# A batch's first expert block: transposed in one slot, begun in the next

## The chip, the cores and the metric

The kernel runs on one core of a Trainium2 chip. Its time is the device time of one execution in microseconds (us). The kernel before takes 1374.13 us (median of three runs, 1373.11 to 1375.44). One further execution was recorded by the hardware profiler: its span from first to last instruction is 1370.3 us. All times with a position ("at 509.0 us") are counted from the start of that span.

The engines are named as in the profile: PE is TensorE (matmuls; PEld its weight loads), DVE is VectorE, ACT is ScalarE, POOL is GpSimd, SP is SyncE. Each works through its own list of instructions in the order in which the kernel issued them.

## The reference

Two stages follow each other: attention in which every query keeps its 32 highest scores, and a mixture of experts in which every token goes to one of eight two-layer networks.

```python
# q, k, v: (8 batches, 8 heads, 576 positions, 64)
scores = scale * np.matmul(q, k.transpose(0, 1, 3, 2))
kth = np.partition(scores, -32, axis=-1)[..., -32:-31]
scores = np.where(scores >= kth, scores, -1000000000.0)
attn = softmax(scores)
attn_out = np.matmul(attn, v)                    # -> x: (4608 tokens, 512)
# experts: w1 (8, 512, 1024), w2 (8, 1024, 512)
logits = x @ w_gate
expert_idx = np.argmax(logits, axis=1)
gate_w = probs[np.arange(N), expert_idx]         # softmax of the logits
y[token] = relu(x[token] @ w1[e]) @ w2[e]        # e = expert_idx[token]
out = gate_w[:, None] * y
```

All of it is in 32-bit floats. The tokens of one expert are gathered into blocks of 128 rows.

## The kernel before

The attention is cut into 144 *slots*, 18 for each of the eight batches. A slot handles two tiles of 128 query rows. I write 3.13 for slot 13 of batch 3. DVE searches the 32 highest scores of slot i; ACT and POOL make the softmax weights from them; PE transposes the weights of slot i-1 and computes the scores of slot i+4 (`AHEAD` is 3).

The experts' work is laid between. When a batch is done, its rows are written to memory, sorted by expert, and the blocks that are full by then are announced. Each block is cut into 16 *pieces*: 8 for the first layer (4 matmuls by 128 columns each) and 8 for the second. A credit counter says how many pieces a slot may do. What is left at the end runs alone on PE.

```python
def turned(n):                               # transpose a block's 128 rows
    ...
        ps = k.ps_m.tile([P, DT, P], F32, name="xtp", tag="m")
    for dt in range(DT):
        nc.tensor.transpose(ps[:, dt, :], n.x[:, 0, dt * P:(dt + 1) * P], ident)
    n.xT = k.mlp.tile([P, DT, P], F32, name="xTs")
    due.append(("xT", lambda: nc.scalar.copy(n.xT, ps)))

def evacuate(upto=None):                     # issue the copies out of PSUM that are due
    while due and (upto is None or upto in [kind for kind, _ in due]):
        due.pop(0)[1]()

def block(n, following=..., put_off=...):
    if not hasattr(n, "xT"):
        turned(n)
        yield "pause"
    evacuate("xT")
    hT = ...
    for half in range(2):
        ...
        for f in range(FT // 2):
            ...                              # 4 matmuls into ph, from n.w1 and n.xT
            yield
    evacuate("h0")
    following()                              # transposes the next block's rows
    yield "pause"
    evacuate()
    for f in range(FT):
        ...                                  # matmuls into py, from hT and n.w2
    ...                                      # y = py * gate weight; store y

def landed(n):                               # loaded at least ON_CHIP = 3 slots ago
    return clock is None or clock - n.at >= ON_CHIP

def following():
    put_stores()
    if loaded and landed(loaded[0]):
        turned(loaded[0])

def pieces(n):                               # do up to n pieces
    nonlocal current, left
    while n > 0 and left > 0:
        if current is None:
            if not landed(loaded[0]):
                break
            current = block(loaded.pop(0), following, stores.append)
            ahead()                          # load the next block
        ...
        step = next(current)
        if step == "pause":
            if clock is not None:            # within the attention
                break
            continue
        if step == "last":
            current = None
        n -= 1
        left -= 1
    return n
```

The slot itself, cut to the order in which PE and ACT get their instructions:

```python
for i, (b, g) in enumerate(work):
    ...
    low, nbias, doubts = search(tiles, s_of[i], f_of.pop(i), then)   # DVE; low on ACT
    w_of[i] = depths(s_of[i], low)               # ACT  L370
    less(s_of.pop(i), w_of[i])                   # POOL L379
    ...
    s_of[i + AHEAD], steps = scores(...)         # ACT  L283, copies the scores
    evacuate()
    turns = turning(i - 1) if i else iter(())
    next(turns, None)                            # PE wTm L398, then ACT copies L404 or L402
    part = min(BETWEEN, now - now // 2)          # BETWEEN = 2
    rest = pieces(part)                          # first call
    next(turns, None)                            # PE wTl L411
    rest = pieces(now - now // 2 - part + rest)  # second call
    weights(tiles, w_of[i], nbias)               # ACT  L387, the exponentials
    next(turns, None)                            # ACT  L419, copies wTl
    evacuate()
    if i + AHEAD + 1 < len(work):
        multiply(i + AHEAD + 1)                  # PE sc L276
    ...                                          # at some slots PE po L432 or px L443
    credit = min(credit + pieces(now // 2 + rest), 6 * rate)   # third call
```

`wTm` and `wTl` share two PSUM banks: `wTl` can begin only when the first ACT copy of `wTm` has freed one. The expert matmuls (`xtp`, `ph`, `py`) have two further banks.

Of the kernel before, what the change touches and what calls it, by code (L numbers as in the profile page):

```python
# [35 lines left out]
def kernel(  # L36
# [203 lines left out]
    def bank(name):  # L240
        return k.ps_t.tile([P, SM], F32, name=name, tag="t")
# [5 lines left out]
    def open_unit(n):  # L247
        n.z = k.small.tile([P, NT], F32, name="z")

    def tails(tiles):  # L250
        return tiles[0][1] == 2 * NC
# [27 lines left out]
    def scores(got):  # L279

        s = k.att.tile([P, 2, 2, HF], F32, name="s", bufs=2 if k.exact else 4)
        return s, [
            lambda m=m, ps=ps: nc.scalar.copy(s[:, m, :, :], ps[:, :, 0:HF]) for m, ps in enumerate(got)  # L283
        ]

    def fold(s):

        f = SimpleNamespace()
        f.h = k.att.tile([P, 2, HF], F32, name="h", bufs=1)
        nc.vector.tensor_tensor(f.h, s[:, :, 0, :], s[:, :, 1, :], op=ALU.max)  # L290
        f.l = k.att.tile([P, 2, HF], F32, name="l")
        nc.vector.tensor_tensor(f.l, s[:, :, 0, :], s[:, :, 1, :], op=ALU.min)
        return f

    def fold_on(f):

        f.few = k.att.tile([P, 2, LW], F32, name="few", bufs=3)
        nc.vector.tensor_tensor(f.few[:, :, 0:QF], f.h[:, :, 0:QF], f.h[:, :, QF:HF], op=ALU.max)
        f.hl = k.att.tile([P, 2, QF], F32, name="hl", bufs=1)
        nc.vector.tensor_tensor(f.hl, f.h[:, :, 0:QF], f.h[:, :, QF:HF], op=ALU.min)  # L300
# [354 lines left out]
    def turned(n):  # L655

        if k.apart:
            ps = bank("xtp")[:, :].rearrange("p (t r) -> p t r", t=DT)
        else:
# [5 lines that stand above are left out]
# [3 lines left out]
    def evacuate(upto=None):  # L668

        while due and (upto is None or upto in [kind for kind, _ in due]):  # L670
            due.pop(0)[1]()
# [62 lines left out]
    with fast:  # L734
# [9 lines left out]
        waiting, loaded, coming, spare, scatters, stores = [], [], [], [], [], []  # L744
        current = None
        left = clock = 0

        def landed(n):
            return clock is None or clock - n.at >= ON_CHIP

        def ahead():
            while waiting and len(loaded) < 2:
                expert, piece = waiting.pop(0)
                if isinstance(piece, SimpleNamespace):
                    rows_in = piece
                elif isinstance(piece, tuple):
                    rows_in = load_rows(SimpleNamespace(), *piece, full=True)
                else:
                    rows_in = load_rows(SimpleNamespace(), piece)
                loaded.append(load_weights(rows_in, expert))  # L760
                loaded[-1].at = clock

        def put_stores():
            while stores:
                stores.pop(0)()

        def following():
            put_stores()
            if loaded and landed(loaded[0]):
                turned(loaded[0])  # L770

        def pieces(n):
            nonlocal current, left
            while n > 0 and left > 0:
                if current is None:
                    if not landed(loaded[0]):
                        break
                    current = block(loaded.pop(0), following, stores.append)
                    ahead()
                if clock is None:  # L780
# [3 lines that stand above are left out]
                    if clock is not None:  # L784
# [7 lines that stand above are left out]
# [90 lines left out]
        def at_place(name):  # L882
            for end in list(late):
                if end[1] == name:
                    end[1] = next(end[0], None)
                    if end[1] is None:
                        late.remove(end)
# [3 lines left out]
        def tiles_of(i):  # L891
            b, g = work[i]
            return [(unit[b * U + u], tile) for u, tile in g]
# [4 lines left out]
        def multiply(i):  # L898
            tiles = tiles_of(i)
            got_of[i] = products(tiles)  # L900
            n, tile = tiles[0]
            more = n.b * U + n.u + 2
            if tile == (NC - 1 if n.u % 2 else 2 * NC) and more < len(units):
                unit.append(load_unit(*units[more]))

        def loop():
            nonlocal credit, rate, clock
            for i in range(min(AHEAD, len(work))):
                multiply(i)
                s_of[i], steps = scores(got_of.pop(i))  # L910
                for step in steps:
                    step()
            multiply(AHEAD)
            f_of[0] = fold(s_of[0])
            fold_on(f_of[0])
            for i, (b, g) in enumerate(work):
                tiles = tiles_of(i)
                u, tile = g[0]
                if tile == 0 and u % 2 == 0:
                    open_unit(tiles[0][0])  # L920
                if tails(tiles):
                    open_unit(tiles[1][0])

                then = lambda: None
                if i + 1 < len(work):
                    f_of[i + 1] = fold(s_of[i + 1])
                    then = lambda: fold_on(f_of[i + 1])
                low, nbias, doubts = search(tiles, s_of[i], f_of.pop(i), then)
                at_place("small")
                w_of[i] = depths(s_of[i], low)  # L930
                less(s_of.pop(i), w_of[i])
                doubts()
                put_stores()
                scatter(1)
                at_place("pool")
                at_place("relu")
                at_place("rows")
                at = i % per_batch
                if at == FIRST and b:
                    rate = new_of[b - 1] * PIECES / (U * NT)  # L940
                credit += rate * len(g)
                room = left
                if b == B - 1 and at >= ARRIVED:
                    room -= KEEP
                    credit = room / (len(work) - i)
                share = {0: 0.5, 1: 1.2, 2: 1.6, 3: 0.5, 2 * NC: 1.4}[tile]
                now = max(0, min(int(credit * share + 0.5), room))
                credit -= now
                clock = i
                if i + AHEAD < len(work):  # L950
                    s_of[i + AHEAD], steps = scores(got_of.pop(i + AHEAD))
                    for step in steps:
                        step()
                evacuate()
                at_place("turn")
                turns = turning(i - 1) if i else iter(())
                next(turns, None)
                part = min(BETWEEN, now - now // 2)
                rest = pieces(part)
                next(turns, None)  # L960
                rest = pieces(now - now // 2 - part + rest)
                weights(tiles, w_of[i], nbias)
                next(turns, None)
                evacuate()
                if i + AHEAD + 1 < len(work):
                    multiply(i + AHEAD + 1)
                if tile == NC - 1:
                    end = ending(b, u)
                    late.append([end, next(end)])
                at_place("products")  # L970
                at_place("weights")
                credit = min(credit + pieces(now // 2 + rest), 6 * rate)

            for _ in turning(len(work) - 1):
                pass
            assert len(late) == 1
            clock = None
            for place in late[0][0]:
                if place == "rows":
                    pieces(4)  # L980
            kept = left - ALWAYS * PIECES
            assert kept >= 0, kept
            k.apart = True
            pieces(kept)
# [135 lines left out]
```

## Time and profile before

| engine | busy in the whole span, us | share |
|---|---|---|
| PE | 1234.6 | 90% |
| DVE | 1084.5 | 79% |
| ACT | 932.0 | 68% |
| POOL | 661.5 | 48% |

The profile's rows name a line of the kernel (L687), an engine, an operation, its output and input tiles, how often it ran, its busy time and its mean duration; behind the second bar stands how long the engine was idle ahead of it, and who released it. The span has two parts: to about 1100 us the 144 slots, in which DVE is busy nearly throughout, and then some 250 us in which PE works off the remaining blocks alone.

### The profile page before, as it was taken

The numbers are of one execution on the slowest core, as the hardware profiler recorded it, in microseconds if no ns is written. First come the engines' busy times: TensorE is split into PE (matmuls) and PEld (weight loads), VectorE is DVE, ScalarE is ACT, GpSimd is POOL, SyncE is SP. The second block draws the span as 40 slices with busy tenths as digits, with TensorE's granted clock in tenths as the row PEclk, the third lists the DMA queues.
The fourth block names the chain that finished last, engine by engine and source line by source line (L and its number), as shares of the span: only waits on it lengthen the run. The fifth ranks groups of instructions, "written<-read, shape, count | busy, mean of one in ns | idle before, by whom it ended". The sixth has DMA issues, their size and how long they took to land. (4 is left out here: it accounts for less than half of the span.)

```text
span 1370.3 us, 24487 instructions
## 1 busy us (share of the span) xinstructions
PE 1234.6 (90%) x7666; PEld 838.6 (61%) x7666; DVE 1084.5 (79%) x4591; ACT 932.0 (68%) x2113; POOL 661.5 (48%) x805
## 2 busy tenths in 40 slices
PE   5777677687799999999999999999999999999995
PEld 3444444344466666766666666767676677776773
DVE  8999999999999999999999999999999820000000
ACT  4788877877888888888877788887777821111110
POOL 3455557555654666566556665565557621000000
PEclk8788787877999999999999999999999999999998
DMA  2100011001583267427654474357542859999880
GB/s 82 29 29 29 28 36 56 29 29 44 178 296 124 89 232 266 142 72 261 226 174 168 166 274 148 113 188 293 184 167 75 308 183 358 390 325 331 301 321 18
DMA packets 102220, 231.68 MB, mean 169 GB/s; under 512 B 5182, under 2 KB 25918, under 8 KB 102080
## 3 DMA queue, kind: packets, MB, share of 16 engines
q1 hardware_dynamic: 95328, 209.76, 43.8%
q0 software_dynamic: 6464, 19.97, 4.0%
q8 instruction: 62, 1.02, 0.3%
q14 instruction: 78, 0.64, 0.1%
q10 hardware_dynamic: 288, 0.30, 0.1%
HBM read 208.72 MB, written 22.33 MB: 169 GB/s over the span
## 5 line engine op out<-in xcount | busy, mean ns | idle before, releaser
L379 POOL TENSOR_TENSOR w<-s,w 128x576 f32<-128x576 f32 x288 | 409.5, 1442 | 432.3 <-ACT w L370 432.3
L687 PE MATMUL ph<-xTs,w 128*128 128x128 f32 x2560 | 308.6, 276 | 6.0 <-ACT xTs L664 6.0
L687 PEld LDWEIGHTS ph<-xTs,w 128*128 128x128 f32 x2560 | 297.4, 192 | 26.4 <-issue 19.1
L702 PE MATMUL py<-w,hT 128*128 128x512 f32 x640 | 292.2, 596 | 0.0
L338 DVE MAX8 tops<-scr 128x8 f32<-128x168 f32 x864 | 245.5, 316 | 0.0
L276 PE MATMUL sc<-qkb 64*128 64x288 f32 (+1 forms) x1280 | 221.6, 472 | 9.5 <-ACT s L283 5.2
L387 ACT ACTIVATE w<-w,nbias 128x576 f32<-128x576 f32 x288 | 224.0, 792 | 3.5 <-POOL w L379 2.5
L370 ACT ACTIVATE w<-s,low 128x576 f32<-128x576 f32 x288 | 207.6, 768 | 4.7
L398 PE MATMUL wTm<-turn,w 128*128 128x128 f32 x1152 | 171.2, 289 | 29.0 <-ACT xl L450 17.7
L398 PEld LDWEIGHTS wTm<-turn,w 128*128 128x128 f32 x1152 | 133.1, 146 | 89.6 <-issue 35.4
L999 DVE CAST any_i<-pd 1x1 int32<-1x1 f32 x1 | 0.1, 146 | 236.0 <-PE pd L997 236.0
L702 PEld LDWEIGHTS py<-w,hT 128*128 128x128 f32 x640 | 114.4, 190 | 117.6 <-issue 116.5
L345 DVE MATCH_REPLACE8 scr<-tops,scr 128x168 f32<-128x168 f32 x576 | 176.9, 311 | 0.0
L283 ACT COPY s<-sc 128x576 f32<-128x576 f32 x288 | 169.1, 641 | 10.5 <-PE sc L276 10.5
L404 ACT COPY wT<-wTm 128x512 f32<-128x512 f32 x256 | 139.1, 604 | 38.9 <-PE wTm L398 38.6
L276 PEld LDWEIGHTS sc<-qkb 64*128 64x128 f32 (+1 forms) x1280 | 118.2, 195 | 72.9 <-issue 26.6
L432 PE MATMUL po<-wT,vb 128*64 128x288 f32 x1024 | 157.8, 457 | 0.4 <-ACT wTt L419 0.4
L708 POOL DMA_INDIRECT out_dram<-y,xg x40 | 43.1, 1078 | 211.9 <-ACT y L716 199.8
L329 DVE MAX8 few<-l 128x8 f32<-128x288 f32 x288 | 127.2, 442 | 0.0
L432 PEld LDWEIGHTS po<-wT,vb 128*64 128x64 f32 x1024 | 75.3, 152 | 78.0 <-issue 29.3
L692 ACT ACTIVATE hT<-ph 128x512 f32<-128x512 f32 x80 | 48.6, 608 | 107.3 <-PE ph L687 107.3
L290 DVE TENSOR_TENSOR h<-s 128x576 f32<-128x576 f32 x144 | 117.0, 812 | 5.8 <-ACT s L283 5.8
(116 smaller groups left out, 1433.4 us busy)
## 6 DMA issues: line engine op xcount, KB each, us to landing
w<-in_moe_w_dram SPq DMA_DIRECT2D x80, 2048.0 KB, 9.6
qkb<-in_qk_dram SPq DMA_DIRECT2D x31, 608.0 KB, 4.3
xg<-x_rows SPq DMA_DIRECT2D x40, 257.0 KB, 10.0
vb<-in_v_dram SPq DMA_DIRECT2D x32, 320.0 KB, 3.2
x_rows<-blank SPq DMA_DIRECT2D x5, 257.0 KB, 14.7
x_rows<-blank POOLq DMA_DIRECT2D x4, 257.0 KB, 8.5
x_rows<-x,posi POOLq DMA_INDIRECT x40, 3.1
out_dram<-y,xg POOLq DMA_INDIRECT x40, 6.1
```

What stands on the lines that cost most here:

```text
L276: nc.tensor.matmul(ps[rows, j, 0:HF], n.q[d, cols], n.k[d, keys], start=True, stop=True)
L283: lambda m=m, ps=ps: nc.scalar.copy(s[:, m, :, :], ps[:, :, 0:HF]) for m, ps in enumerate(got)
L338: nc.vector.max(out=tops[:, m, r * 8:(r + 1) * 8], in_=src[m])
L345: nc.vector.match_replace(out=scr[:, m, :], in_to_replace=tops[:, m, r * 8:(r + 1) * 8], in_values=src[m], imm_value=NEG,)
L370: nc.scalar.activation(w[:, m, :], s[:, m, :, :].rearrange("p j k -> p (j k)"), AF.Relu, scale=-STEEP, bias=low[:, m:m + 1],)
L379: k.last_pool = in_turn(nc.gpsimd.tensor_tensor(w[:, m, :], s[:, m, :, :].rearrange("p j k -> p (j k)"), w[:, m, :], op=ALU.subtract)).ins
L387: nc.scalar.activation(w[:, m, :], w[:, m, :], AF.Exp, scale=scale, bias=nbias[:, m:m + 1], accum_out=n.z[:, c:c + 1])
L398: nc.tensor.transpose(pm[:, c * P:(c + 1) * P], w[:, m, first:first + P], ident)
L404: nc.scalar.copy(wT[:, :, m, q], pm4)
L432: nc.tensor.matmul(po[r, 0:HF], n.v[:, c, r], rhs, start=(c == 0), stop=(c == KC - 1))
L687: nc.tensor.matmul(ph[:, f, :], n.w1[:, 0, dt, fc * P:(fc + 1) * P], n.xT[:, dt, :], start=(dt == 0), stop=(dt == DT - 1),)
L702: nc.tensor.matmul(py, hT[:, f, :], n.w2[:, 0, f, :], start=(f == 0), stop=(f == FT - 1))
```

## The change

Inside the attention, a block may now begin only in a slot later than the one in which its rows were transposed. To make that possible, a slot in which no block is in progress transposes the rows of the next loaded block near its end, and the `evacuate()` behind it copies them out of PSUM. The change is for the first block of each batch: there no earlier block runs that could call `following()` for it, so the kernel before transposes, copies and multiplies within one slot.

```diff
         def following():
             put_stores()
-            if loaded and landed(loaded[0]):
+            if loaded and landed(loaded[0]) and not hasattr(loaded[0], "xT"):
                 turned(loaded[0])
+                loaded[0].turned = clock
 
         def pieces(n):
             nonlocal current, left
             while n > 0 and left > 0:
                 if current is None:
-                    if not landed(loaded[0]):
+                    if clock is not None and getattr(loaded[0], "turned", clock) == clock:
                         break
@@ in the slot @@
                 rest = pieces(now - now // 2 - part + rest)
                 weights(tiles, w_of[i], nbias)
                 next(turns, None)
+                if current is None:
+                    following()
                 evacuate()
                 if i + AHEAD + 1 < len(work):
                     multiply(i + AHEAD + 1)
```

## The prediction

> **What bounds the kernel now.** I read the busy table by engine first. No single row answers the question, because the span has two parts, so I asked for windows of time. The columns are PE, PEld, DVE, ACT, POOL busy, then the granted PE clock and DMA. The four windows are batches 3 to 6; I set their edges at the start of DVE's first operation of the batch (L290).
>
> ```profile
> 399.50:531.90 132.40, 129.12 (x869) 89.51 (x869) 132.40 (x572) 111.75 (x257) 77.43 (x94) 1.00 0.52 181
> 531.90:667.60 135.70, 132.01 (x874) 90.31 (x873) 134.48 (x573) 113.88 (x260) 83.00 (x98) 1.00 0.50 178
> 667.60:812.90 145.30, 144.07 (x963) 100.72 (x962) 141.93 (x573) 115.50 (x265) 87.04 (x99) 1.00 0.56 198
> 812.90:948.50 135.60, 131.91 (x873) 90.27 (x872) 134.39 (x572) 113.86 (x260) 82.93 (x98) 1.00 0.50 178
> ```
>
> See two things. PE and DVE are both near full, so neither alone is the bound. And a batch takes longer the more pieces it carries: 132.4 us with 64 pieces, 135.7 with 68, 145.3 with 76 (the counts are worked out below). DVE has the same 573 instructions in the third window as in the second, yet is "busy" 7.5 us longer: its instructions get longer, which I come back to.
>
> Then the waits (total us, times, longest), for what the change aims at:
>
> ```profile
> DVE h L290 <- ACT s L283: 5.8, 6, 1.5
> PEld ph L687 <- ACT xTs L664: 7.3, 6, 1.3
> PE ph L687 <- ACT xTs L664: 6.0, 6, 1.1
> PE wTl L411 <- ACT wT L404: 67.1, 61, 3.9
> ```
>
> Six waits of PE for the copy of the transposed rows, 6.0 us together: one for each batch from the third on that starts a block cold. That is 0.44% of 1374 us, and the most that taking these waits away can bring. The timeline of PE at the second of them, slot 3.13:
>
> ```profile
> 506.37 1.22 PE L398 MATMUL wTm<-turn,w 128*128 128x128 f32 x8
> 507.43 1.02 PE L702 MATMUL py<-w,hT 128*128 128x512 f32 x2
> 508.29 0.60 PE L662 MATMUL xtp<-turn,xg 128*128 128x128 f32 x4
> 508.73 0.27 PE L411 MATMUL wTl<-turn,w 128*128 128x128 f32 x1
> 510.06 2.05 PE L687 MATMUL ph<-xTs,w 128*128 128x128 f32 x16 [1.06 <-ACT xTs L664]
> 512.04 1.24 PE L276 MATMUL sc<-qkb 64*128 64x288 f32 x8
> 513.22 2.94 PE L687 MATMUL ph<-xTs,w 128*128 128x128 f32 x24
> 516.00 1.04 PE L398 MATMUL wTm<-turn,w 128*128 128x128 f32 x8
> ```
>
> Start, duration, what, how many. The last piece of the old block (py), the transposes, wTl, 1.06 us of nothing, two pieces, the scores, three pieces, and slot 3.14 begins at 516.00. Three pieces take 513.22 to 516.00: 0.93 us a piece. ACT over the same time:
>
> ```profile
> 508.80 0.73 ACT L716 ACTIVATE y<-py,xg 128x512 f32<-128x512 f32 x1
> 509.38 0.63 ACT L664 COPY xTs<-xtp 128x512 f32<-128x512 f32 x1
> 511.82 1.44 ACT L370 ACTIVATE w<-s,low 128x576 f32<-128x576 f32 x2
> 513.48 1.15 ACT L283 COPY s<-sc 128x576 f32<-128x576 f32 x2
> 516.63 0.59 ACT L402 COPY wT<-wTm 128x512 f32<-128x512 f32 x1 [0.73 <-PE wTm L398]
> ```
>
> Both copies stand ahead of the exponentials. At the end ACT waits for PE, not PE for ACT: here PE is the later one.
>
> **What the Trainium skill says.** "Perfetto Trace Analysis", section "Per-instruction lifecycle", says that ACT, DVE and GpSimd are strict first-in first-out, so a copy queued ahead of the exponentials delays them. The order of ACT above agrees: y 508.80, xTs 509.38, then the rest. The same page, "Identifying the Most-Contended Engine", warns that matmul busy time does not say how far PE is from its limit; I therefore count PE's idle stretches and its lateness, not its 98%. "SBUF — State Buffer", section "Who interferes with whom", says that a DVE instruction with two SBUF inputs contends with a GpSimd instruction that reads SBUF. The trace agrees for some: from 340 us on the two-input L298 takes 0.44 us when POOL is idle, and 0.92 on average (up to 1.38) in the 18 cases that overlap most with POOL's L379; L290 goes from 0.73 to 1.69 in four such cases. (L292, with two inputs too, stays at 0.74.) So lateness of PE costs in two ways: ACT copies the scores late and DVE waits, and POOL's L379 slides onto DVE's two-input instructions.
>
> **The change part by part.** First the counting, which needs no time. Following `credit`, `share`, `now`, the pauses and `ON_CHIP` through all 144 slots gives the pieces done in the three calls of every slot. With the code before, blocks start cold at 2.13, 3.13, ... 7.13, which fits the six waits, and the trace shows 2 and then 3 pieces after the cold start at 3.13, as counted. Slots 13 to 17:
>
> | batches | before | after |
> |---|---|---|
> | 2 | 0+3+2, 1, 2+0+4, 2+0+2, 1 | 0, 2+0+2, 2+2+0, 2+3+5, 0 |
> | 3, 5 | 1+2+3, 1, 2+0+4, 2+0+2, 1 | 1, 2+0+2, 2+2+0, 2+3+5, 0 |
> | 4, 6 | 1+3+4, 1, 0+3+3, 2+1+3, 1 | 1, 2+0+2, 2+2+7, 2+0+2, 1+0+1 |
> | 7 | 1+2+2, 1+0+1, 2, 2+1+3, 1 | 1, 1+0+1, 2+1+3, 0+3+3, 1 |
>
> Sums over the attention: 367 pieces before, 367 after; 273 remain for afterwards in both. So the tail of some 250 us doesn't change, and neither do the numbers of matmuls, transposes, copies and transfers. What moves is five to eight pieces: out of slot 13, and most of them into slot 15 or 16, which then has 10 or 11 pieces, 9 to 10 us of PE on top of its attention work.
>
> *Removed:* 0.65 us at 2.13 (from the timeline at 375 us) and 1.06 us at each of the other five, 5.95 us of PE.
>
> *Added at 3.13,* step by step from the timeline. py and wTl end at about 508.7, as no transposes stand between; scores 1.2 to 509.9; transposes 0.5 to 510.4; then wTm of slot 14. ACT ends the exponentials (0.77 + 0.77) that now come straight behind the wT copies at 510.4, wTl copy 510.7, y 511.3, xTs 511.9. So the first pieces of slot 14 (wTm done at 511.5) wait 0.5 us for xTs after all: "the slot behind" is only microseconds away for an engine that has nothing else. They end at 513.85. Then wTl needs ACT's wT copy, and ACT has before it: low 0.25, L370 1.44, two rz copies 0.4, the scores 1.15. From 511.9 that is 515.1, and the first wT copy ends at 515.75. PE is idle for 1.9 us. Then scores 1.2, po 2.6 and two pieces 1.85: slot 15 begins at 521.7 us with 5 pieces done since 3.13 began; before it begins at 521.82 (L398 in the timeline) with 7. Two pieces, 1.85 us, are owed. That is 2.4 added less 1.06 removed, and about 0.4 of rounding.
>
> *Added at the bump.* Slot 15 (4 pieces, px 1.3) ends at about 529.9; slot 16 takes 2.5 for wTm, wTl and scores and 10 x 0.92, so slot 17 begins near 541.6 where before it begins near 537.0. In slot 17 there is no piece ahead of wTl, which then waits about 0.3 us (the 0.24 to 0.31 that such slots show). At slot 4.0 PE is some 3 us late with one piece more than before: about 2 us net.
>
> *Sum.* At 3.13, 4.13, 5.13 and 6.13 about -1.06 + 0.5 + 1.9 + 0.3 = +1.6 each; at 7.13, where slot 14 gets one piece only in the first call, about +0.5; 2.13 lies where DVE sets the pace (3.35 us PE wait just before it), about 0. Together +7 us of PE lateness. Not all reaches the end: PE also waits for latency elsewhere (1.1 us for oT in batches 3, 4 and 6), and DVE, less held up in slots 14 and 15 (the slots from 4.16 on last 8.2, 8.0, 9.1, 8.8 us against 7.03 undisturbed), gets a start on the bump. I count 40% of it, a choice: +3 us, or 1377 us.
>
> **The rivals.** (a) The waits are simply gone: 1374 - 6 = 1368. For it: PE is the late engine in batches 4 to 7, and its own idle time there is lost time. Against it: the same ACT chain (exponentials, two copies, low, L370, scores, wT) has to be passed by PE with fewer pieces to fill it. (b) The wait moves: xTs and wTl in slot 14 take its place, and the bump makes PE late at 16 and 17: 1377, up to 1384 if every bump also stalls DVE by the 3 us that I get for slot 4.2 when PE's scores come at 543 and ACT needs until 549 to copy them, where DVE wants them at 546. (c) All is hidden, because DVE is the bound: 1374. DVE's lowest batch (131 us without the pieces' disturbance) against PE's 132 in batch 3 speaks for it there, the 145 us of batch 5 against it. (d) Weight loads: a block is taken one slot later, so the load behind it is issued later. But its buffer is free only when the block before is done, and a block's weights are asked for at least three slots, 21 us, ahead of their use: no effect.
>
> **Range and chances.** The terms are known to 1 us each, six times, with either sign: 1369 to 1385 should hold it. 2% is 27 us, more than four times all the waits concerned: faster by that 1%, slower by that 2%, within 97%.
>
> **What would show it.** In the changed profile: no six waits of ph for xTs of 1.06 us at cold starts, or fewer and shorter ones in slot 14; the wait of wTl for ACT's wT copy up by some 5 to 10 us in sum from 67.1; batches 3, 5 with DVE slots near 7.03 at 14 to 16 and stretched ones at 17 to 2; the tail unchanged to 1 us. If wTl doesn't wait at slot 14, the wait is removed for nothing and (a) holds. If DVE's stretches shrink in batches 4 to 6, I have weighed the bump too heavily.

## The result, and the profile after

The changed kernel takes 1384.7 us (median of four runs, 1383.26 to 1385.71) against 1374.43. The ratio is 1.0075, with a 95% interval from 1.0057 to 1.0092: about 10 us slower. The prediction was 1377 us, 1369 to 1385.

First the waits of the changed kernel, in the view used before (total us, times, longest):

```profile
PE wTl L411 <- ACT wT L404: 68.0, 60, 3.7
PE wTl L409 <- ACT wT L402: 20.4, 9, 3.8
PE ph L687 <- ACT xTs L664: 1.3, 5, 0.3
DVE h L290 <- ACT s L283: 9.1, 6, 2.4
```

The kernel before had one line of these that was not shown:

```profile
PE wTl L409 <- ACT wT L402: 8.5, 3, 3.0
```

The wait for the copied rows (xTs) fell from 6.0 to 1.3 us, as intended. The wait of wTl for ACT's copy of wTm rose by 11.9 us, 10.1 of it in six new places: slot 14 of batches 2 to 7. L409 and L402 are the forms of wTl and of that copy in a slot that follows a *tail slot* (its tiles hold the last 64 query rows of two heads), and slot 14 is one.

The timeline of PE over slots 3.13 and 3.14 in the changed kernel:

```profile
511.17 1.23 PE L398 MATMUL wTm<-turn,w 128*128 128x128 f32 x8
512.23 1.02 PE L702 MATMUL py<-w,hT 128*128 128x512 f32 x2
513.31 0.33 PE L411 MATMUL wTl<-turn,w 128*128 128x128 f32 x1
513.48 0.60 PE L662 MATMUL xtp<-turn,xg 128*128 128x128 f32 x4
514.01 1.24 PE L276 MATMUL sc<-qkb 64*128 64x288 f32 x8
515.18 1.09 PE L398 MATMUL wTm<-turn,w 128*128 128x128 f32 x8
516.53 2.05 PE L687 MATMUL ph<-xTs,w 128*128 128x128 f32 x16 [0.26 <-ACT xTs L664]
519.96 0.41 PE L409 MATMUL wTl<-turn,w 128*64 128x128 f32 x2 [1.38 <-ACT wT L402]
```

and of ACT over the same time:

```profile
515.86 0.62 ACT L664 COPY xTs<-xtp 128x512 f32<-128x512 f32 x1
516.61 1.44 ACT L370 ACTIVATE w<-s,low 128x576 f32<-128x576 f32 x2
518.27 1.15 ACT L283 COPY s<-sc 128x576 f32<-128x576 f32 x2
519.32 1.06 ACT L402 COPY wT<-wTm 128x512 f32<-128x512 f32 x2
```

Slot 3.13 lasts 4.0 us on PE instead of 9.6, because it holds one piece instead of six. So PE reaches slot 3.14 while ACT still has L370, the score copies and more ahead of the copy that frees a bank for wTl. Two pieces do not cover that, and PE stands idle for 0.26 + 1.38 us, where before it stood idle for 1.06.

To see where the whole 10 us are, I cut the attention at the starts of PE's slots 2.13, 3.13, ... 7.13 and at the last wTm. The columns are the stretch, its length, PE busy (instructions), granted clock, the busy share of the DMA engines and their GB/s. First and last stretch of the kernel before:

```profile
372.34:506.37 134.03, 130.68 (x874) 1.00 0.52 180
1068.35:1099.35 31.00, 28.66 (x195) 1.00 0.71 266
```

First, second and last stretch of the changed kernel:

```profile
371.98:511.17 139.19, 132.45 (x874) 0.99 0.51 178
511.17:647.17 136.00, 131.84 (x877) 1.00 0.50 177
1078.40:1111.34 32.94, 30.36 (x195) 0.95 0.64 242
```

The same numbers of matmuls take longer. All six stretches:

| stretch from | before, us | after, us | difference |
|---|---|---|---|
| 2.13 | 134.03 | 139.19 | +5.16 |
| 3.13 | 134.34 | 136.00 | +1.66 |
| 4.13 | 146.65 | 147.61 | +0.96 |
| 5.13 | 134.33 | 136.01 | +1.68 |
| 6.13 | 146.66 | 147.61 | +0.95 |
| 7.13 | 31.00 | 32.94 | +1.94 |
| sum | 727.01 | 739.36 | +12.35 |
| of it PE idle | 15.52 | 22.53 | +7.01 |
| of it PE busy | 711.49 | 716.83 | +5.34 |

The two profiled executions differ by 13.8 us, of which 12.35 lie here; of the rest, 1.7 us are waits of PE for transfers in the tail. The first row also holds 1.7 us that come from the cut alone. In slot 2.12 PE's clock is halved in the profile before and full in the one after, so PE passes the mark at 2.13 earlier and then waits. DVE's search is the better mark: its slots last 7.02 to 7.09 us in both kernels from 2.10 to 2.16. First the po matmuls of slot 2.12, then DVE's first instruction of slot 2.13, each before and after:

```profile
368.07 3.85 PE L432 MATMUL po<-wT,vb 128*64 128x288 f32 x16
369.41 2.16 PE L432 MATMUL po<-wT,vb 128*64 128x288 f32 x16
363.25 0.74 DVE L290 TENSOR_TENSOR h<-s 128x576 f32<-128x576 f32 x1
364.58 0.73 DVE L290 TENSOR_TENSOR h<-s 128x576 f32<-128x576 f32 x1
```

Counted from there, PE begins slot 3.13 after 143.12 us before and 146.59 after, 3.47 us later, and the last wTm comes 10.65 us later. That fits the 10 us of the timed runs.

That PE is *busy* longer with as many matmuls has a visible part. At 2.14 and 7.14 the wait for wTl lasts 2.28 and 2.27 us. Behind the first of them the granted clock falls (2 us a line, the third value from the end):

```profile
382.00:384.00 2.00, 1.68 (x12) 0.96 1.00 394
384.00:386.00 2.00, 2.00 (x10) 0.50 1.04 389
386.00:388.00 2.00, 2.00 (x14) 0.69 1.05 389
```

The 16 po matmuls there take 3.83 us, and 3.45 at 7.14, where they take 2.16 at full clock (all in the timeline of PE): 1.67 + 1.29 = 3.0 us of the 5.34. Behind the waits of 1.38 us the clock stays at 1.00.

### The profile page after: what moved, and what is told of

The parts are those of the page before. It is cut to its first block, busy times and chain, and to the rows that moved or that the text cites. A ratio compares the mean times of both kernels' runs of the same rounds, so it can differ in the third digit from the quotient of the medians.

```text
span 1384.1 us, 24489 instructions
## 1 busy us (share of the span) xinstructions
PE 1236.2 (89%) x7666; PEld 839.2 (61%) x7666; DVE 1079.2 (78%) x4591; ACT 930.6 (67%) x2113; POOL 652.7 (47%) x805
## 5 line engine op out<-in xcount | busy, mean ns | idle before, releaser
L379 POOL TENSOR_TENSOR w<-s,w 128x576 f32<-128x576 f32 x288 | 406.1, 1430 | 453.3 <-ACT w L370 453.3
L370 ACT ACTIVATE w<-s,low 128x576 f32<-128x576 f32 x288 | 207.7, 768 | 4.7
```

The source lines that it names most:

```text
L370: nc.scalar.activation(w[:, m, :], s[:, m, :, :].rearrange("p j k -> p (j k)"), AF.Relu, scale=-STEEP, bias=low[:, m:m + 1],)
L379: k.last_pool = in_turn(nc.gpsimd.tensor_tensor(w[:, m, :], s[:, m, :, :].rearrange("p j k -> p (j k)"), w[:, m, :], op=ALU.subtract)).ins
```

## The experiments

At the time of the first four runs I held the crowded slots 15 and 16 (theory A), the idle time of PE in slots 13 and 14 (B) or the place of the copies (C) for possible causes. Each ratio is to the kernel before on the same chip, with its 95% interval.

**e1, no slot lost.** Transposed at the end of slot 13, begun in the third call of the same slot.

```diff
-  if clock is not None and getattr(loaded[0], "turned", clock) == clock:
+  if clock is not None and not hasattr(loaded[0], "xT"):
```

> The early transposition stays, but the block may begin in the third call of the same slot, so that no slot is lost: slot 13 does 0+0+5 or 1+0+5 or 1+0+7 pieces, all later slots have the counts of the kernel before. Theory A (the crowded slot 15 or 16 with 10 or 11 pieces holds DVE up): at or below before, 1368 to 1374 us, DVE slot 1 of batches 3, 4 and 6 back near 7.0 us from 10.6. Theory B (PE stands idle in slots 13 and 14 for want of pieces): the same, at or below 1374. Theory C (the place of the transposes and of the copies behind the exponentials costs the time): still 1380 or more.

1373.51 us, ratio 1.0001 (0.9993 to 1.0010). Theory C falls. But nothing is gained either: at five of the six starts PE now waits 1.28 us for xTs, behind the scores, as the copy stands behind the exponentials and y in ACT's list. (Its line in the timeline: ph at 512.73 [1.28 <-ACT xTs L664].)

**e2, the delay without the early transposition.** The kernel before, with a cold start one slot later.

```diff
-  if not landed(loaded[0]):
+  n0 = loaded[0]
+  cold = not hasattr(n0, "xT")
+  if not landed(n0) or cold and clock is not None and clock - n0.at <= ON_CHIP:
       break
```

> The kernel before with its cold start (transpose, pause and first pieces in one slot), only one slot later: the slots 14 to 17 have the counts of the changed kernel. Theory A: 1383 to 1388 us, with DVE slot 1 of batches 3, 4 and 6 at 10 us or more. Theory B: 1380 to 1386. Theory C: within 3 us of before.

1400.88 us, ratio 1.0196 (1.0182 to 1.0210): far above every expectation. The slot counts are those of the change, so a theory of crowded slots alone can't give 16 us more than the change. The profile can: between 2.13 and the last wTm PE is idle for 32.2 us against 22.5 with the change. In slot 3.14 there is no piece at all ahead of wTl, which waits 2.92 us, and ph another 0.55; behind it the clock is halved, at every start:

```profile
518.00:522.00 4.00, 1.08 (x10) 1.00 1.02 410
522.00:524.00 2.00, 1.45 (x9) 0.82 1.03 387
524.00:526.00 2.00, 2.00 (x11) 0.50 1.05 388
```

**e3, the crowded slots evened out.** The change, with at most 6 pieces in a slot from 14 on.

```diff
   now = max(0, min(int(credit * share + 0.5), room))
+  if at > FIRST:
+      now = min(now, 6)
```

> The changed kernel, but no slot from 14 on takes more than 6 pieces: what is owed from slot 13 is spread over slots 16 to 2 of the next batch. The empty slot 13 and the PE waits of slots 13 and 14 stay. Theory A: 1377 us or less, DVE slot 1 near 7.0 in batches 3, 4 and 6. Theory B: 1382 or more, as the idle time of PE is untouched. In the kernel before this cap never binds, so before is its own control.

1381.18 us, ratio 1.0049 (1.0035 to 1.0063): between the two expectations. DVE's slot 3.1, 10.63 us in the change, is back at 7.08, and PE's stretch from 3.13 falls from 136.00 to 134.76. The waits of slot 14 are unchanged there (0.26 + 1.38 us). So DVE's long slot is mostly a sign that PE is late, and the crowding is worth some 3 us (1.2 us in each of the stretches from 3.13 and 5.13, 0.2 from 4.13 and 6.13). What is gained lies in the slots beside the crowded one, 17 and 0, which get pieces for the first call; there wTl's waits of 0.24 and 0.30 us are gone.

**e4, only the first start delayed.**

```diff
   if current is None:
+      if not landed(loaded[0]):
+          break
-      if clock is not None and getattr(loaded[0], "turned", clock) == clock:
+      if clock is not None and clock // per_batch == 2 and getattr(...) == clock:
...
-  if current is None:
+  if current is None and i // per_batch == 2:
       following()
```

> Only the first start (2.13) is delayed by a slot; later batches start cold as before. My prediction gave this start nothing, as PE has slack there: 1374 us. Theory A: the crowded slot 2.16 holds DVE up whether or not PE had slack before it, 4 to 5 us: 1378 to 1379, with DVE slot 3.1 at 10.6 us.

1376.74 us, ratio 1.0025 (1.0018 to 1.0032), +3.1 us; in the profiled execution the stretch from 2.13 is 5.13 us longer and all others are as before to 0.01 us. So the start to which my prediction gave nothing is no free one. Why 3.1 and not 5.1: 1.7 us are the cut, as above. Counted from DVE's mark, PE begins slot 3.13 3.4 us later than before. The cost also varies: with the same instructions, slot 2.14 lasts 12.8 us in the profiles of the change and of e4 but 10.2 in that of e3, where wTl waits 1.33 us instead of 2.28 and the clock does not fall. (e3's five times form two groups, 1378.0 and 1381.2 to 1381.7 us, and the profiled one is of the first; that the fall parts them is not shown.)

After these I held theory D: from slot 2.13 on PE always has expert pieces to do, so each microsecond in which it is idle, or at half clock, is lost, whatever DVE does.

**e5, copy ahead of the exponentials.** e1, with transposes and copies moved up.

```diff
+  if current is None:
+      following()
+      evacuate()
   weights(tiles, w_of[i], nbias)
   next(turns, None)
-  if current is None:
-      following()
   evacuate()
```

> As the same-slot kernel, but transposes and copy stand ahead of the exponentials, so that ACT has copied the rows while PE does the scores; the pieces of slot 13 follow in its third call. No slot is lost. Theory D (from slot 2.13 on PE always has expert work waiting, so each microsecond in which it stands idle is lost one to one): the six waits for the copy, 6 to 7 us, are gone and nothing takes their place: 1367 to 1369 us. Rival (DVE's slots set the pace and waits of PE are free): 1373 to 1374.

1368.84 us, ratio 0.9966 (0.9954 to 0.9978): 4.5 us faster than the kernel before, and so faster than both. The timeline of PE at 3.13:

```profile
509.52 1.02 PE L702 MATMUL py<-w,hT 128*128 128x512 f32 x2
510.60 0.33 PE L411 MATMUL wTl<-turn,w 128*128 128x128 f32 x1
510.76 0.60 PE L662 MATMUL xtp<-turn,xg 128*128 128x128 f32 x4
511.29 1.24 PE L276 MATMUL sc<-qkb 64*128 64x288 f32 x8
512.46 4.73 PE L687 MATMUL ph<-xTs,w 128*128 128x128 f32 x40
```

The 1.2 us of scores cover the copy, and no wait is left. PE's idle time between the marks is 10.9 us against 15.5.

**e6, only the last start delayed.** As e4, with batch 7 for batch 2.

> Only the last start (7.13) is delayed. My prediction gave it 0.5 us. Theory D, from the profile of the changed kernel: 1.06 us of wait removed, 0.26 + 2.27 us of idle added and 1.3 us because the granted clock is halved behind the long idle stretch: about 2 us in all, 1375.5 to 1376.5.

1376.60 us, ratio 1.0022 (1.0012 to 1.0032), +3.3 us, a little over. The profile shows 2.06 us from 7.13 on, as expected, and 0.85 us more in the stretch ahead of it: the rule also holds back a block at 7.1, whose rows are transposed in that very slot, within the run of the block before it.

**e7, the change with its copy ahead of the exponentials.** The same move as in e5, in the changed kernel.

> The change itself, with transposes and copy ahead of the exponentials. The 0.26 us waits for the copied rows in slot 14 go. Theory D: PE reaches the next wait, for the copy of wTm, earlier by as much and waits longer there, because ACT sets that time: within 1.5 us of the changed kernel, 1383 to 1386 us. Rival (the late copy is what costs): 1379 or less.

1384.00 us, ratio 1.0079 (1.0066 to 1.0092), no different from the change. The waits of slot 14 moved:

```profile
PE wTl L409 <- ACT wT L402: 16.1, 9, 3.7
PE wTm L398 <- ACT w L387: 2.2, 6, 0.4
PE wTm L398 <- ACT wTt L419: 1.5, 6, 0.3
```

At 3.14 they are 0.38 for the exponentials, 0.25 for wTl's copy and 0.99 for wTm's: 1.62 us where the change has 0.26 + 1.38 = 1.64. ACT sets the time, and PE meets it at one wait or another.

**e8, e5 with at most 7 pieces in any slot.** One line, `now = min(now, 7)`.

> The copy-first kernel with at most 7 pieces in any slot: the crowded slots 5.1, 5.4, 7.1 and 7.4 with 8 or 9 pieces are evened out. Theory D: the number of pieces is the same and PE is bound, so at most the 0.2 to 0.3 us waits of slots without a piece in the first call change: within 2 us of the copy-first kernel. If crowded slots cost by themselves: 2 to 4 us faster than it.

1370.52 us, ratio 0.9979 (0.9970 to 0.9988): not faster than e5. Slots with 8 or 9 pieces cost nothing here by being crowded.

**e9, slot 14 filled where PE waits.** The change; slot 14 does its pieces all in the first call.

```diff
-  part = min(BETWEEN, now - now // 2)
+  part = now if at == FIRST + 1 else min(BETWEEN, now - now // 2)
```

> The change, but slot 14 does all its pieces (4, at 7.14 two) in its first call, ahead of wTl, where PE otherwise waits for ACT's copy of wTm. The delay by a slot, the empty slot 13 and the crowded slots 15 and 16 stay. Theory D: the waits of 1.4 us (five starts, 2.3 us at the first and the last) shrink to under 0.5 us, and where the clock was halved behind them it stays full: 8 to 10 us faster than the change, 1375 to 1377 us. Rival (the delay or the crowded slots cost by themselves): 1381 or more.

1374.38 us, ratio 1.0004 (0.9996 to 1.0012). The delay by a slot, the nearly empty slot 13 and the 10 or 11 pieces of slot 15 or 16 are all still there, and the 10 us are gone. The timeline of PE in slot 3.14:

```profile
514.00 3.84 PE L687 MATMUL ph<-xTs,w 128*128 128x128 f32 x32 [0.26 <-ACT xTs L664]
517.68 0.38 PE L409 MATMUL wTl<-turn,w 128*64 128x128 f32 x2
```

Four pieces instead of two stand ahead of wTl, and it waits no longer. At 7.14, with two pieces ahead instead of one, it still waits 1.38 us, not less than 0.5 as I expected. The clock stays full behind 2.14 and 7.14.

So these waits and the clock are worth the 10 us. They are not all that the delay costs: the six waits of 1.06 us are gone here as in e5, and yet e5 is 5 us faster by the ratios. Between the marks e9 has 3.7 us more of idle time than e5 (the 1.38 us above, 0.26 at five starts, 0.79 and 0.69 for wTm in 2.15 and 7.15, less what e5 has elsewhere) and 2.8 us more of busy time. The crowded slots' 3 us of e3 may be part of this; that they are is not shown.

**e10, the rule for starts only.** The change, but rows transposed within a running block may be used in the same slot.

```diff
-  loaded[0].turned = clock
+  loaded[0].turned = clock if current is None else -1
```

> The change, but its rule holds only for rows transposed at the end of a slot, not for those transposed within a running block; so the blocks at 5.1 and 7.1 may begin in the slot of their transposes as before. Theory D, from the two stages of the only-batch-7 run: 0.85 us each at 5.1 and 7.1, together 1 to 2 us faster than the change, 1382.5 to 1384 us; all starts at slot 13 as in the change.

1383.70 us, ratio 1.0075 (1.0061 to 1.0089). In the profile both stretches, from 4.13 and from 6.13, are 0.85 us shorter than with the change (146.76 for 147.61). In the timed runs the 1.0 us is within the spread of either kernel, so this one is inconclusive as a time.

All idle times of PE together with the length of the same part (PE's 2.13 to the last wTm), how much later than before the last wTm comes when counted from DVE's 2.13, and the time of the kernel:

| kernel | part, us | PE idle, us | last wTm, us later | timed, us |
|---|---|---|---|---|
| e5 copy first | 722.1 | 10.9 | -3.7 | 1368.8 |
| e8 copy first, at most 7 | 723.6 | 11.8 | -3.5 | 1370.5 |
| before | 727.0 | 15.5 | 0 | 1374.4 |
| e1 same slot | 728.5 | 17.3 | 2.2 | 1373.5 |
| e9 slot 14 filled | 728.6 | 14.6 | 1.6 | 1374.4 |
| e6 only 7.13 | 729.9 | 16.4 | 2.9 | 1376.6 |
| e3 capped | 731.7 | 18.3 | 5.4 | 1381.2 |
| e4 only 2.13 | 732.1 | 18.9 | 3.4 | 1376.7 |
| e7 change, copy first | 735.3 | 21.0 | 8.2 | 1384.0 |
| e10 starts only | 736.3 | 19.9 | 9.3 | 1383.7 |
| the change | 739.4 | 22.5 | 10.7 | 1384.7 |
| e2 cold, later | 756.4 | 32.2 | 27.7 | 1400.9 |

The part follows the idle time, to within a few us, and grows beyond it where the clock falls (e2: 12.8 us of PE busy more than before). The profiled execution of e3 and that of e7 are the fastest of their five (1377.95 and 1379.62 us) and that of e1 the slowest of its 13 (1375.92), so their parts look short and long beside the median.

## Why the prediction was right, and what in it was not

*The mechanism held.* Rival (b), "the wait moves", was the prediction, and that is what happened: xTs 6.0 to 1.3 us, wTl's wait for ACT up instead, in slot 14. At 3.14 I had worked out 0.5 + 1.9 us; measured are 0.26 + 1.38. e9 shows that this is the cause of the 10 us and not an accompaniment: with these waits filled and all else left, the time is that of before, though not that of e5.

*The estimate for 3.13 and 5.13* was +1.6 us each; the stretches grew by 1.66 and 1.68. For 4.13 and 6.13, also put at 1.6, it was 0.96 and 0.95. Of each of these 0.85 belongs to the blocks held back at 5.1 and 7.1 (e10), so those two starts cost 0.1 us each.

*The step that failed is the sum's treatment of three terms.* First, "2.13 lies where DVE sets the pace, about 0": it cost 3.5 us in the profile, counted from DVE's mark, and 3.1 in the timed runs of e4. The slack that I saw there (3.35 us of wait just before) is not slack to spend. Slot 2.13 is where pieces begin to fill it, and PE is late from batch 3 on; five pieces taken out of idle time are done later in time that PE doesn't have. Second, 7.13 was put at 0.5 us and cost 1.94, as its slot 14 has one piece only ahead of wTl. Third, "I count 40% of it": all of it reaches the end, as e5 shows in the other direction (4.6 us of idle time less in the profile, 4.5 us less in the timed runs). My four terms of 1.6 us, taken in full and with 3.5 for 2.13 and 1.94 for 7.13 as measured, would have given 11.8 us, beside 10.65 in the profile and 10.3 in the timed runs. Some of that closeness is luck: the terms for 4.13 and 6.13 were too large by 1.5 us each, and the halved clock and the blocks at 5.1 and 7.1 were not in the sum. That the range held is in part luck too: one of the four timed runs, 1385.71 us, lies beyond its upper end.

*One term was missing:* the clock that is halved behind the waits at 2.14 and 7.14, about 3 us of the 12.35.

*The bump* was over-weighted as a cause and right as a sight: DVE's slot 1 of batches 3, 4 and 6 did last 10.6 us (I had 3 us of stall at 4.2, it is 3.6 at 4.1), but e9 keeps the crowded slot without the loss of 10 us, and e8 gains nothing by evening out slots of 8 or 9 pieces; the 3 us that e3 gains come from slots of 10 or 11. The second route of cost, POOL's L379 sliding onto DVE's instructions, went the other way: DVE is busy 705.8 us between the marks against 710.6.

*Right:* the tail did not change because of the change (from the last wTm to the end 270.95 us before, 272.76 after, 270.98 in e9); PE waits for no transfer of weights within the attention; the 367 pieces are where the table put them (by which slot 13 loses four to seven pieces, not "five to eight"). *Not foreseen:* that the rule also holds back blocks at 5.1 and 7.1, 0.85 us each in the profile.

*Open:* of the 5.34 us by which PE is busy longer, 3.0 are the halved clock at 2.14 and 7.14; the other 2.3 are spread over all stretches (0.1 to 0.7 each) and I did not follow them to instructions.

## What to carry to other kernels

Where one engine is the last to finish over a long stretch, its idle time just before and inside that stretch is where work must go, not slack that can be given away: taking work out of a slot opens the next in-order wait behind it. Before delaying work to avoid a wait of 1 us, look for other work of the same slot that can stand in front of the wait (here 1.2 us of scores) and put the copy that is waited for early in its engine's list. And a change of order has to be read in the idle time of the bound engine, not in the count of waits of the kind that was meant.

## What the hardware showed unexpectedly

PE's granted clock fell to half after a single wait of 2.27 or 2.28 us between matmuls (for 3.41 us, with 1.3 to 1.7 us lost by the po matmuls), and after 2.92 us at each of five starts in e2; after 1.38 us it never did. The Trainium skill ("TensorE: Matmul & The Clock Gate", section "What's actually happening") states that the clock halves after at least one idle window of about 3.4 us. Here 2.3 us of standing still were enough, with PE busy only 1.66 us of the 4 us from 1083 to 1087; the measurement decides.

The length of the wait alone does not settle it. In e10 the clock fell at 2.14 after a wait of 1.78 us, and in e7 it stayed full at 7.14 after one of 1.88. Each trace's changes of the clock lie whole multiples of 3.41 us apart. Here is such a stretch and the one behind it, in e10 and then in e7:

```profile
380.70:384.12 3.42, 1.64 (x15) 1.00 1.03 406
384.12:387.53 3.41, 3.41 (x16) 0.50 1.02 389
1081.20:1084.61 3.41, 1.53 (x14) 1.00 1.03 405
1084.61:1088.02 3.41, 3.34 (x26) 1.00 1.04 386
```

Over all twelve traces, no stretch at full clock in which PE was busy for less than 1.5 us (as the profile counts it) was without a fall behind it, and none with more than 2.0 us had one. Between the two either can happen. So whether a wait of about 2 us costs only itself or also half the clock for 3.41 us depends on how it lies across these stretches, which begin at other moments in every execution.
